# A blocked attention and two MLPs on one core: the y product three steps behind h, and small VectorE work moved to ScalarE and GpSimd

## The chip, the cores and the metric

The kernel runs on one core of a Trainium2 chip. The metric is the device time of one execution in microseconds. The core has TensorE (matmuls, and its weight loads, PE and PEld in the profile), VectorE (DVE), ScalarE (ACT), GpSimd (POOL) and SyncE (SP, which here only sends DMAs). Each engine works through its own instructions in order; semaphores order them against each other.

## The reference

```python
# q, k, v: 2 x 8 heads x 768 x 64; 8 global keys, a local window of 96
scores = scale * np.matmul(q, k.transpose(0, 1, 3, 2))
...
scores = np.where(keep, scores + bias, -1000000000.0)
scores = scores - np.max(scores, axis=-1, keepdims=True)
a = np.exp(scores)
a = a / (np.sum(a, axis=-1, keepdims=True) + 1e-09)
x = np.matmul(a, v)                    # then 1536 tokens x 512
h = x @ w_in                           # first MLP, 512 -> 2048
x = (h * np.cos(h)) @ w_out
g = x @ w_gate                         # second MLP, 512 -> 1536
out = (g * (1.0 / (1.0 + np.exp(-g))) * (x @ w_val)) @ w_out
```

`keep` lets through the global keys and those at most 95 positions back.

## The kernel before

**Numbers.** Every large product is made of three matmuls on halves: a tensor is split into a high part (a copy on ScalarE to a matmul format, `split_hi`) and a low part (what is left, a subtraction on VectorE or GpSimd, `split_lo`), and high x high, high x low and low x high are summed in PSUM. The weights come as 64-bit numbers; `narrow` makes 32-bit ones of them with three integer instructions on VectorE (L183, L186, L193), called a conversion here. A conversion is done once for each 512-column piece, the split anew for each block of tokens.

**Stages.** The tokens are in three blocks of 512. Attention of the first four tiles of 128 tokens runs alone (the prologue). The first MLP runs over 48 steps, 16 for each block; in the first 32 (`for s in range(last)`), the attention of the other eight tiles is woven in at fixed steps (`steady`, with the constants at the top of the file, `BASES` and others). What is written there is put in order on each engine by a scheduler that works before the kernel runs. From the last block of the first MLP on, the order is as written. The second MLP takes 36 steps.

**A step of the first MLP.** `h_mm(s)`: twelve matmuls into one of two PSUM buffers of tag h. `chain_a`: k, the nearest whole number of h/2pi, on ScalarE. `chain_f`: f, what is left, on VectorE (L311). `chain_sin`: sine and square on ScalarE (L320, L321). `chain_c`: the product with h, in place in PSUM, on VectorE (L328), and its high part g on ScalarE (L332). `chain_d`: the low part of g, on VectorE (L338), which is the last reader of the h buffer. `y_mm(s)`: twelve matmuls with w_out. In a step s, `h_mm(s)` comes first, then `y_mm(s - 2)`, then the chain of step s - 1. In steps 0 to 15 the weights of step s + 2 for h and of step s + 1 for y are fetched, and those of s + 2 and s converted.

**A tile of attention.** Scores, their maxima on VectorE (`scores_max`), the negated maxima (`neg_max`, L838, 128x8), exponentials with their sums on ScalarE, a split of the result (`split_p`), DMA transposes sent by SyncE (L865), the product with v (`pv`), and `x_norm`: reciprocals of the sums times v's scales (r, L899, 128x8), and the product of that with x into xn (L901). TensorE turns xn (`x_turn`, L220). In the prologue |v| is summed as well (`v_scale_part`), for the scales.

**Pools.** SBUF: `ch` holds f and k, two buffers each, `g` two buffers, `xn` one, `vr` two (v as loaded). In the second MLP, `silu` writes into f's buffers, `act` into g's, and the output tiles use k's and f's. A tile that takes a buffer waits until the last reader of the one before is done. All DMAs but one go through SyncE's queue, in order, and one that waits holds up those behind.

Of the kernel before, what the change touches and what calls it, by code (L numbers as in the profile page):

```python
# [22 lines left out]
P = 128  # L23
# [18 lines left out]
SP = (7, 7, 8, 8)  # L42
PVS = (10, 11, 11, 11)
XN = 13
XE = 15
# [8 lines left out]
E4 = 2  # L54
LAG = 2
VB = 5
VBE = 7
# [12 lines left out]
def attention_moe_moe2_kernel(  # L70
# [175 lines left out]
    def first_mlp(c1, before, steps, last_block):  # L246
# [60 lines left out]
        def chain_f(s):  # L307
            n = BLOCKS[todo[s][0]][1]
            h, k = hs[s]
            f = ch_p.tile([P, 512], F32, tag="f", name="f")  # L310
            nc.vector.scalar_tensor_tensor(  # L311
                out=f[:, :n], in0=h[:, :n], scalar=INV2PI, in1=k[:, :n],
                op0=ALU.mult, op1=ALU.subtract,
            )
            fs[s] = f
# [49 lines left out]
        def begin():  # L365
            get("i", 0)
            get("i", 1)
            get("o", 0)
            use("i", w_in, 0)
            use("i", w_in, 1)  # L370
            prep_in(0)

        before(hp, begin, prep_in, h_early)
        ch_p = c1.enter_context(tc.tile_pool(name="ch", bufs=2))
        g_p = c1.enter_context(tc.tile_pool(name="g", bufs=2))
        yp = c1.enter_context(tc.tile_pool(name="yp", bufs=4, space=PSUM))
        last = nsteps - NF1
        for s in range(last):
            early, late = steps.get(s, ((), ()))
            if s < NF1:  # L380
                get("i", s + 2)
                get("o", s + 1)
            ps = h_mm(s)
            if s >= 2:
                y_mm(s - 2)
# [8 lines left out]
            if s < NF1:  # L394
                use("i", w_in, s + 2)
                use("o", w_out, s)
            prep_out(s - 1)
            chain_a(s, ps)
# [50 lines left out]
    def second_mlp(c2, ch_p, g_p, hp, yp):  # L449
# [51 lines left out]
        def silu(s):  # L501
            n = BLOCKS[todo[s][0]][1]
            sl = ch_p.tile([P, 512], F32, tag="f", name="sl")
            nc.scalar.activation(out=sl[:, :n], in_=ps_.pop(("g", s))[:, :n], func=AF.Silu)  # L504
# [15 lines left out]
        def o_mm(s):  # L520
# [5 lines left out]
            for m in range(nt // P):  # L526
# [8 lines left out]
                if j == NF2 - 1:  # L535
                    end = b == len(BLOCKS) - 1
                    o = ch_p.tile([P, DM], F32, tag="kf"[end and m // 2], name="osb")
                    rows = slice(t0 + m * P, t0 + (m + 1) * P)
# [56 lines left out]
    def windowed_path():  # L595
# [7 lines left out]
        with ExitStack() as ca:  # L603
# [42 lines left out]
            pt_p = ca.enter_context(tc.tile_pool(name="pt", bufs=4, side="right"))  # L646
            xn_p = ca.enter_context(tc.tile_pool(name="xn", bufs=1, side="right"))
            sm_p = ca.enter_context(tc.tile_pool(name="sm", bufs=2, side="right"))
# [187 lines left out]
            def neg_max(i, p0, p1):  # L836
                c = slice(2 * p0, 2 * p1)
                nc.vector.tensor_scalar(  # L838
                    T["nm", i][:, c], T["mx", i][:, c], -1.0, P_SHIFT * LN2,
                    op0=ALU.mult, op1=ALU.add,  # L840
                )
# [49 lines left out]

            def x_norm(i):
                b = i // TB
                r = sm_p.tile([P, H], F32, tag="r", name="r")
# [3 lines left out]
                nc.vector.reciprocal(out=r, in_=r)  # L898
                nc.vector.tensor_tensor(out=r, in0=r, in1=vsc[b][:, H:2 * H], op=ALU.mult)  # L899
                xn = xn_p.tile([P, DM], F32, tag="xn", name="xn")  # L900
                nc.vector.tensor_tensor(  # L901
# [15 lines left out]
            def steady(i):  # L917
# [25 lines left out]
                for p in range(4):  # L943
                    add(SP[p] // 2, SP[p] % 2, split_p, i, p, eng(PLE, 4 * i + p), nc.scalar.copy)
                    add(PVS[p] // 2, PVS[p] % 2, pv, i, p)
                add(XN // 2, XN % 2, x_norm, i)
                add(XN // 2, L, x_tr, i)
# [22 lines left out]
            def prologue(hp, begin, prep_in, h_early):  # L970
                with (
# [31 lines left out]
                    for w in range(NW + LAG + 2):  # L1003
# [37 lines left out]
                        if 0 <= w - LAG < NW:  # L1041
                            i, pp = pairs[w - LAG]
                            pv(i, 2 * pp)
                            pv(i, 2 * pp + 1)
                            if pp == 1:
                                x_norm(i)
                        if 0 <= w - LAG - 1 < NW:
# [154 lines left out]
```

## Time and profile before

| | |
|---|---|
| time, three runs | 715.47, 719.28, 720.06 us; median 719.28 |
| profiled execution | 716.73 us, span 715.0 |
| mean granted TensorE clock | 0.972 |
| TensorE busy | 662.3 us, 93% of the span |
| VectorE busy | 483.9 us, 68% |
| ScalarE busy | 394.7 us, 55% |
| GpSimd busy | 115.3 us, 16% |

The span runs from the first to the last instruction; the profiled execution's own time lies 1.7 us above it. Busy shares are means over stages that have different limits, so they are to be read by stretch. The granted clock is a share of full speed.

### The profile page before, as it was taken

The page shows a single profiled execution, that of the slowest core. Times are in us where ns is not written, and L with a number is a line of the kernel's source. Part 1 is how long each engine was busy: PE and PEld are TensorE (multiplying, and loading weights), DVE is VectorE, ACT ScalarE, POOL GpSimd, SP SyncE. Part 2 cuts the span into 40 slices and gives each one's busy share as a digit, 9 for nine tenths or more (in the row PEclk, how much of TensorE's full clock was granted, in tenths as well). Part 3 has the DMA queues.
Part 4 walks back from the last instruction along what each step waited for, and adds up shares of the span by engine and source line. Part 5 has one row for each costly group of instructions (what it writes and reads, how often), then busy time and mean ns, then how long its engine had stood idle before and what let it go on. Part 6 is the DMA issues. An engine that isn't in the chain of part 4 may idle for free.

```text
span 715.0 us, 9068 instructions
## 1 busy us (share of the span) xinstructions
PE 662.3 (93%) x3276; PEld 521.5 (73%) x3276; DVE 483.9 (68%) x886; ACT 394.7 (55%) x820; POOL 115.3 (16%) x108
## 2 busy tenths in 40 slices
PE   4777898987898999999999999999999999999997
PEld 3345676756676777787888888888888888888885
DVE  4795999989987566747999869878443444433442
ACT  5566678777486898766666743332333333333331
POOL 2564333523322332420000000000000000000000
PEclk9996799998999999999999999999999999999999
DMA  6788546648534122300332224542000000100001
GB/s 222 190 195 211 170 132 224 172 130 201 136 104 68 37 49 45 60 1 30 102 104 89 88 59 126 161 126 88 30 30 0 1 1 0 60 0 1 1 0 63
DMA packets 69652, 62.73 MB, mean 88 GB/s; under 512 B 48896, under 2 KB 55296, under 8 KB 69600
## 3 DMA queue, kind: packets, MB, share of 16 engines
q1 hardware_dynamic: 69456, 61.95, 31.4%
q8 instruction: 27, 0.44, 0.2%
q14 instruction: 25, 0.20, 0.1%
q10 hardware_dynamic: 144, 0.13, 0.1%
HBM read 47.19 MB, written 3.15 MB: 70 GB/s over the span
## 4 chain that ended last, share of the span: by engine, by line
PE 65%; DVE 16%; ACT 10%; DMA 4%; issue 2%; POOL 1%; SPq 0%; DVEq 0%; ACTq 0%; POOLq 0%
PE v L492 14%; PE o L528 14%; PE g L492 14%; PE h L274 10%; PE y L350 10%; DMA pt<-ph 3%; ACT sb L848 3%; DVE w L193 2%; DVE w L186 2%; DVE sb L830 1%; PE s L778 1%; DVE w L183 1%; ACT L320 1%; ACT L848 1%; DVE h L328 1%
## 5 line engine op out<-in xcount | busy, mean ns | idle before, releaser
L210 DVE TENSOR_TENSOR ws<-w,ws 128x512 fp32r<-128x512 f32 x161 | 112.6, 720 | 95.1 <-ACT ws L206 94.9
L350 PE MATMUL y<-g,ws 128*128 128x512 f32 x576 | 145.8, 399 | 12.9 <-ACT g L332 11.4
L274 PE MATMUL h<-xh,ws 128*128 128x512 f32 (+1 forms) x392 | 136.3, 409 | 3.9 <-ACT xh L225 2.2
L350 PEld LDWEIGHTS y<-g,ws 128*128 128x128 f32 x576 | 109.1, 191 | 39.2 <-ACT g L332 10.9
L206 ACT CAST ws<-w 128x512 fp32r<-128x512 f32 x204 | 121.9, 615 | 21.1 <-DVE w L193 13.3
L528 PE MATMUL o<-ws,a 128*128 128x512 f32 x432 | 104.7, 391 | 0.0
L492 PE MATMUL v<-xh,ws 128*128 128x512 f32 x288 | 96.3, 395 | 0.0
L274 PEld LDWEIGHTS h<-xh,ws 128*128 128x128 f32 x392 | 77.4, 200 | 24.5 <-DVE g L338 3.6
L492 PE MATMUL g<-xh,ws 128*128 128x512 f32 x288 | 94.7, 390 | 0.0
L528 PEld LDWEIGHTS o<-ws,a 128*128 128x128 f32 x432 | 81.1, 188 | 18.4
L274 PE MATMUL h<-xl,ws 128*128 128x512 f32 (+1 forms) x196 | 78.8, 402 | 0.0
L210 POOL TENSOR_TENSOR ws<-w,ws 128x512 fp32r<-128x512 f32 x43 | 60.3, 1403 | 109.6 <-ACT ws L206 98.6
L504 ACT ACTIVATE sl<-g 128x512 f32<-128x512 f32 x36 | 21.5, 598 | 97.5 <-PE g L492 97.5
L492 PEld LDWEIGHTS v<-xh,ws 128*128 128x128 f32 x288 | 54.2, 188 | 12.7
L514 ACT CAST a<-sl 128x512 fp32r<-128x512 f32 x36 | 22.4, 622 | 72.6 <-DVE sl L510 72.6
L492 PEld LDWEIGHTS g<-xh,ws 128*128 128x128 f32 x288 | 54.1, 188 | 11.2
L492 PE MATMUL v<-xl,ws 128*128 128x512 f32 x144 | 56.9, 395 | 0.0
L492 PE MATMUL g<-xl,ws 128*128 128x512 f32 x144 | 56.0, 389 | 0.0
L193 DVE SCALAR_TENSOR_TENSOR w<-st,w 128x512 int32<-128x512 int32 x68 | 53.9, 802 | 0.8
L186 DVE SCALAR_TENSOR_TENSOR w<-st,w 128x512 int32<-128x512 int32 x68 | 48.6, 723 | 1.2
L300 ACT ACTIVATE k<-h 128x512 int32<-128x512 f32 x48 | 28.4, 592 | 34.4 <-PE h L274 34.3
L311 DVE SCALAR_TENSOR_TENSOR f<-h,k 128x512 f32<-128x512 f32 x48 | 32.9, 685 | 20.8 <-ACT k L300 20.5
(111 smaller groups left out, 821.9 us busy)
## 6 DMA issues: line engine op xcount, KB each, us to landing
st<-w1i SPq DMA_DIRECT2D x16, 512.0 KB, 3.8
st<-w1o SPq DMA_DIRECT2D x16, 512.0 KB, 4.3
st<-w2g SPq DMA_DIRECT2D x12, 512.0 KB, 3.7
st<-w2v SPq DMA_DIRECT2D x12, 512.0 KB, 3.7
st<-w2o SPq DMA_DIRECT2D x12, 512.0 KB, 3.7
vr<-v SPq DMA_DIRECT2D x16, 256.0 KB, 3.8
kr<-kT SPq DMA_DIRECT2D x12, 256.0 KB, 4.1
qr<-qT SPq DMA_DIRECT2D x12, 256.0 KB, 3.4
```

The source lines that it names most:

```text
L186: nc.vector.scalar_tensor_tensor(out=w, in0=hi, scalar=-(1 << 30), in1=w, op0=ALU.bitwise_and, op1=ALU.bitwise_or,)
L193: nc.vector.scalar_tensor_tensor(out=w, in0=lo, scalar=29, in1=w, op0=ALU.logical_shift_right, op1=ALU.bitwise_or,)
L206: nc.scalar.copy(out=s[:, 0, :], in_=w)
L210: e.tensor_tensor(out=s[:, 1, :], in0=w, in1=f32(s[:, 0, :]), op=ALU.subtract)
L274: nc.tensor.matmul(hps[s][:, c0:c1], lhsT=wis[s][:, a, k * P:(k + 1) * P], rhs=xx[:, k, t0 + c0:t0 + c1], start=(k == 0 and a == 0 and xx ...
L300: nc.scalar.activation(out=k[:, :n], in_=ps[:, :n], func=AF.Copy, scale=INV2PI)
L311: nc.vector.scalar_tensor_tensor(out=f[:, :n], in0=h[:, :n], scalar=INV2PI, in1=k[:, :n], op0=ALU.mult, op1=ALU.subtract,)
L350: nc.tensor.matmul(ys[b][m][:, :n], lhsT=w[:, a, m * P:(m + 1) * P], rhs=g[:, c, :n], start=(j == 0 and a == 0 and c == 0), stop=(j == NF1 ...
L492: nc.tensor.matmul(ps[:, :n], lhsT=w[:, a, k * P:(k + 1) * P], rhs=xx[:, k, t0:t0 + n], start=(k == 0 and a == 0 and xx is xh), stop=(k == ...
L514: nc.scalar.copy(out=a[:, 0, :n], in_=sl[:, :n])
L528: nc.tensor.matmul(os_[b][m], lhsT=a[:, c, m * P:(m + 1) * P], rhs=w[:, d, :], start=(j == 0 and c == 0 and d == 0), stop=(j == NF2 - 1 an ...
L848: nc.scalar.activation(out=a, in_=a, func=AF.Exp, bias=nm[:, h:h + 1], accum_out=sm[:, h:h + 1])
```

## The change

Five things. The y product stands three steps behind h up to step 20, where two y follow each other, and two behind from there; the loads, conversions and splits of w_out move one step back with it, and g has three buffers. f has one buffer, xn uses those of vr, `silu` those of k, and three of four output tiles those of g, the fourth that of f. `neg_max` runs on ScalarE. `x_weights` is taken out of `x_norm`, with its product on GpSimd for the eight tiles that are woven in, and stands at a step of its own, 4; in the prologue it stays on VectorE, where it was.

```diff
+RN = 8
...
+CATCH = 20
...
-            f = ch_p.tile([P, 512], F32, tag="f", name="f")
+            f = ch_p.tile([P, 512], F32, tag="f", bufs=1, name="f")
...
             get("i", 0)
             get("i", 1)
-            get("o", 0)
...
-        g_p = c1.enter_context(tc.tile_pool(name="g", bufs=2))
+        g_p = c1.enter_context(tc.tile_pool(name="g", bufs=3))
...
             if s < NF1:
                 get("i", s + 2)
-                get("o", s + 1)
+                get("o", s)
+            elif s == NF1:
+                get("o", s - 1)
             ps = h_mm(s)
-            if s >= 2:
+            if s <= CATCH:
+                if s >= 3:
+                    y_mm(s - 3)
+            if s >= CATCH:
                 y_mm(s - 2)
...
             if s < NF1:
                 use("i", w_in, s + 2)
-                use("o", w_out, s)
-            prep_out(s - 1)
+                if s >= 1:
+                    use("o", w_out, s - 1)
+            elif s == NF1:
+                use("o", w_out, s - 1)
+            if s < CATCH:
+                prep_out(s - 2)
+            if s >= CATCH - 1:
+                prep_out(s - 1)
...
-            sl = ch_p.tile([P, 512], F32, tag="f", name="sl")
+            sl = ch_p.tile([P, 512], F32, tag="k", name="sl")
...
-                    o = ch_p.tile([P, DM], F32, tag="kf"[end and m // 2], name="osb")
+                    if m < 3:
+                        o = f32(g_p.tile([P, 2, DM], F32R, tag="g", name="osb")[:, 0, :])
+                    else:
+                        o = ch_p.tile([P, DM], F32, tag="f", bufs=1, name="osb")
...
-                nc.vector.tensor_scalar(
-                    T["nm", i][:, c], T["mx", i][:, c], -1.0, P_SHIFT * LN2,
-                    op0=ALU.mult, op1=ALU.add,
+                nc.scalar.activation(
+                    out=T["nm", i][:, c], in_=T["mx", i][:, c], func=AF.Copy, scale=-1.0,
+                    bias=P_SHIFT * LN2,
                 )
...
-            def x_norm(i):
-                b = i // TB
+            def x_weights(i, e):
+
                 r = sm_p.tile([P, H], F32, tag="r", name="r")
...
                 nc.vector.reciprocal(out=r, in_=r)
-                nc.vector.tensor_tensor(out=r, in0=r, in1=vsc[b][:, H:2 * H], op=ALU.mult)
-                xn = xn_p.tile([P, DM], F32, tag="xn", name="xn")
+                e.tensor_tensor(out=r, in0=r, in1=vsc[i // TB][:, H:2 * H], op=ALU.mult)
+                T["r", i] = r
+
+            def x_norm(i):
+                r = T.pop(("r", i))
+                xn = vr_p.tile([P, DM], F32, tag="vr", name="xn")
...
+                add(RN // 2, RN % 2, x_weights, i, nc.gpsimd)
...
+                                x_weights(i, nc.vector)
                                 x_norm(i)
```

VectorE's order in the prologue, behind the low part xl of the second tile. Names end in a number for each buffer; w is a weight piece in conversion from st, r the product of reciprocals and scales, qr the queries, vm the maxima of the sums of |v|. Before:

```order
L226 TENSOR_TENSOR xl_107<-xT_629,xh_106 128x4x128
L895 TENSOR_SCALAR r_813<-sum_559 128x8
L898 RECIPROCAL r_813<-r_813 128x8
L899 TENSOR_TENSOR r_813<-r_813,vsc0_138 128x8
L901 TENSOR_TENSOR xn_723<-x_604,r_719 128x512
L695 TENSOR_TENSOR qr_77<-qr_77,hsc_109 128x512
L667 TENSOR_REDUCE vm_676<-vsum_487 128x8
```

After:

```order
L188 SCALAR_TENSOR_TENSOR w_901<-st_861,w_901 128x512
L185 TENSOR_SCALAR w_905<-st_839 128x512
L195 SCALAR_TENSOR_TENSOR w_901<-st_861,w_901 128x512
L188 SCALAR_TENSOR_TENSOR w_905<-st_839,w_905 128x512
L195 SCALAR_TENSOR_TENSOR w_905<-st_839,w_905 128x512
L909 TENSOR_SCALAR r_808<-sum_554 128x8
L912 RECIPROCAL r_808<-r_808 128x8
L709 TENSOR_TENSOR qr_77<-qr_77,hsc_109 128x512
L810 TENSOR_REDUCE mx_721<-s2_724 128x4
L919 TENSOR_TENSOR xn_718<-x_599,r_714 128x512
```

Two conversions now end ahead of xn of the third tile: a fourth piece of w_in (st_861) and the first of w_out (st_839); the first of w_out was converted a little earlier before, the fourth of w_in behind the prologue.

TensorE's order ahead of h of step 6 (h_1272 before, h_1252 after). s are scores of a woven tile; g_1205 is g of step 4, g_1110 that of step 3. Before:

```order
L755 MATMUL s_1307<-kr_76,qr_77 128x128 x2
L350 MATMUL y_942<-g_1205,ws_1217 128x512
L350 MATMUL y_943<-g_1205,ws_1217 128x512
L350 MATMUL y_944<-g_1205,ws_1217 128x512
L350 MATMUL y_945<-g_1205,ws_1217 128x512
L274 MATMUL h_1272<-xh_106,ws_1183 128x512
```

After:

```order
L769 MATMUL s_1287<-kr_76,qr_77 128x128 x2
L352 MATMUL y_981<-g_1110,ws_1197 128x512 x2
L352 MATMUL y_982<-g_1110,ws_1197 128x512 x2
L352 MATMUL y_983<-g_1110,ws_1197 128x512
L352 MATMUL y_981<-g_1110,ws_1197 128x512
L352 MATMUL y_982<-g_1110,ws_1197 128x512
L352 MATMUL y_983<-g_1110,ws_1197 128x512 x2
L352 MATMUL y_984<-g_1110,ws_1197 128x512 x2
L276 MATMUL h_1252<-xh_106,ws_1163 128x512
```

Where the four matmuls with the high part of g of step 4 stood, eleven of the twelve of step 3 stand.

SyncE's queue in the prologue, around the transposes of the third tile (pt<-ph); kr, qr, v and st are loads of keys, queries, v and weights. Before:

```order
L865 DMA_TRANSPOSE pt_502<-ph_499 128x8x128
L865 DMA_TRANSPOSE pt_507<-ph_504 128x8x128
L865 DMA_TRANSPOSE pt_594<-ph_591 128x8x128
L865 DMA_TRANSPOSE pt_599<-ph_596 128x8x128
L702 DMA vr_666<-v 128x512
L702 DMA vr_671<-v 128x512
L110 DMA kr_76<-kT 128x4x128
L865 DMA_TRANSPOSE pt_688<-ph_685 128x8x128
```

After:

```order
L879 DMA_TRANSPOSE pt_499<-ph_496 128x8x128
L879 DMA_TRANSPOSE pt_504<-ph_501 128x8x128
L176 DMA st_861<-w1i 128x1024
L716 DMA vr_572<-v 128x512
L879 DMA_TRANSPOSE pt_589<-ph_586 128x8x128
L716 DMA vr_577<-v 128x512
L879 DMA_TRANSPOSE pt_594<-ph_591 128x8x128
L112 DMA kr_76<-kT 128x4x128
L716 DMA vr_661<-v 128x512
L716 DMA vr_666<-v 128x512
L879 DMA_TRANSPOSE pt_683<-ph_680 128x8x128
```

A load of weights and two of v have come among the transposes; two more of v now stand ahead of the last one shown. vr_577 takes the buffer of the xn of the second tile, vr_666 that of vr_577.

## Rows read from the trace of the kernel before

**Rows 1.** Busy time by stretch: us; PE, PEld, DVE, ACT, POOL busy (instructions); clock, DMA share, GB/s.

```profile
75.95:195.00 119.05, 102.44 (x551) 76.66 (x550) 111.97 (x223) 88.47 (x186) 42.17 (x32) 0.92 0.61 170
195.00:345.00 150.00, 143.32 (x802) 113.02 (x802) 102.41 (x213) 116.48 (x241) 38.16 (x29) 1.00 0.23 50
345.00:715.00 370.00, 364.64 (x1591) 298.58 (x1589) 218.41 (x350) 146.76 (x260) 0.00 (x0) 1.00 0.17 53
```

**Rows 2.** Waits of TensorE, whole span: us in total, times, longest.

```profile
PE y L350 <- ACT g L332: 11.4, 7, 4.2
```

**Rows 3.** Waits of VectorE from 75 to 200 us: the same columns.

```profile
DVE w L183 <- DMA st<-w1i: 3.5, 3, 1.3
```

**Rows 4.** Groups by line to 345 us (count, busy us, mean ns); last, one line's ns min/median/max.

```profile
L899 DVE TENSOR_TENSOR r<-r,vsc 128x8 f32<-128x8 f32 x12 | 7.0, 585 | 0.1
...
L838 DVE TENSOR_SCALAR nm<-mx 128x8 f32<-128x8 f32 x7 | 2.5, 351 | 0.0
...
L311 DVE SCALAR_TENSOR_TENSOR f<-h,k x48: 674/684/693, 76.0 to 404.9; 128x512 f32<-128x512 f32 x48
```

**Rows 5.** Timeline of VectorE: start us, us, what.

```profile
81.41 1.23 DVE L838 TENSOR_SCALAR nm<-mx 128x4 f32<-128x4 f32 x1
82.55 0.68 DVE L311 SCALAR_TENSOR_TENSOR f<-h,k 128x512 f32<-128x512 f32 x1
...
136.24 1.17 DVE L838 TENSOR_SCALAR nm<-mx 128x8 f32<-128x8 f32 x1
...
157.81 0.16 DVE L838 TENSOR_SCALAR nm<-mx 128x8 f32<-128x8 f32 x1
157.88 0.76 DVE L183 TENSOR_SCALAR w<-st 128x512 int32<-128x512 int32 x2
```

**Rows 6.** Timeline of GpSimd.

```profile
81.00 1.61 POOL L210 TENSOR_TENSOR ws<-w,ws 128x512 fp32r<-128x512 f32 x1 [1.77 <-ACT ws L206]
```

**Rows 7.** ScalarE: a table load in its timeline, and its smallest copy by line.

```profile
76.44 1.28 ACT L320 ACT_TABLE_LOAD   x1
...
L685 ACT COPY kr<-gk 128x128 f32<-128x128 f32 x8 | 2.4, 295 | 5.4 <-PE s L778 5.3 <-PE s L755 0.2
```

**Rows 8.** Timeline of VectorE late in the prologue; in brackets the wait before.

```profile
56.82 0.17 DVE L895 TENSOR_SCALAR r<-sum 128x8 f32<-128x8 f32 x1 [0.69 <-ACT sb L810]
57.03 0.20 DVE L898 RECIPROCAL r<-r 128x8 f32<-128x8 f32 x1
...
61.31 0.69 DVE L901 TENSOR_TENSOR xn<-x,r 128x512 f32<-128x512 f32 x1 [3.88 <-PE x L888]
```

**Rows 9.** Timeline of VectorE amid conversions.

```profile
103.96 0.41 DVE L183 TENSOR_SCALAR w<-st 128x512 int32<-128x512 int32 x1
104.29 0.68 DVE L338 TENSOR_TENSOR g<-h,g 128x512 fp32r<-128x512 f32 x1
104.89 0.68 DVE L193 SCALAR_TENSOR_TENSOR w<-st,w 128x512 int32<-128x512 int32 x1
```

**Rows 10.** Timeline of TensorE: one y.

```profile
164.22 2.88 PE L350 MATMUL y<-g,ws 128*128 128x512 f32 x12
```

**Rows 11.** Timeline of VectorE at the end.

```profile
709.00 0.69 DVE L547 COPY osb<-o 128x512 f32<-128x512 f32 x1 [0.67 <-PE o L528]
709.68 0.42 DVE L541 COPY osb<-o 128x256 f32<-128x256 f32 x1
```

**Rows 12.** Timelines of SyncE's queue and of TensorE in the prologue.

```profile
46.00 6.38 SPq L865 DMA_TRANSPOSE pt<-ph  x4
52.44 1.05 SPq L702 DMA_DIRECT2D vr<-v  x2
...
54.35 1.58 SPq L865 DMA_TRANSPOSE pt<-ph  x1
...
50.40 0.64 PE L220 MATMUL xT<-ident,xn 128*128 128x128 f32 x4
```

**Rows 13.** DMA issues by line: KB each, median us to landing.

```profile
vr<-v SPq DMA_DIRECT2D x16, 256.0 KB, 3.8
```

More of the change, by code (lines that the diff above doesn't have):

```diff
@@ L646, in windowed_path @@
             pt_p = ca.enter_context(tc.tile_pool(name="pt", bufs=4, side="right"))
-            xn_p = ca.enter_context(tc.tile_pool(name="xn", bufs=1, side="right"))
             sm_p = ca.enter_context(tc.tile_pool(name="sm", bufs=2, side="right"))
```

## The prediction

> **What bounds the kernel now.** I first cut the span into three stretches [rows 1]. From 75.95 us, where the chain of the first step begins on VectorE, to 195 us, VectorE is busy 111.97 of 119.05 us and TensorE 102.44, at a mean granted clock of 0.92. From 195 to 345 us TensorE is busy 143.32 of 150 us at full clock. Behind 345 us it is busy 364.64 of 370, and the rest is the end of the program. So the change can win only in the first stretch, where VectorE sets the pace, in the 6.7 us that TensorE still waits in the second, and ahead of 75.95 us. The waits of TensorE seem to say otherwise: its longest are for g, 11.4 us in seven waits, the longest 4.2 us [rows 2]. But g is the end of the chain k, f, sine, square, c, g, d, and three of its links run on VectorE. h has two PSUM buffers, and c and d work in them, so h of step s cannot begin before d of step s - 2 is through. Between the end of h(s-2) and the start of h(s), TensorE has one y, one h and one y to do whether y is two steps behind or three; the lag decides only which y that is. A later y is a filler for a short stall, but it does not let the chain start sooner.
>
> VectorE's own losses in the first stretch are of two kinds. It waits for weights, 3.5 us in three waits [rows 3]. And some of its small instructions last far longer than they need: the negation of the maxima has a mean of 351 ns and the product r a mean of 585 ns [rows 4], although an undisturbed negation holds VectorE for 0.07 us (157.81 to 157.88) [rows 5]. A negation that began at 81.41 lasted 1.23 us, to 82.64, and GpSimd worked on a split from 81.00 to 82.61 [rows 5, 6]. Another lasted 1.17 us at 136.24. With two products there are four such in the stretch, each of some 1.1 us more than it needs. By the same views VectorE's f, which reads PSUM and one SBUF tile, never lasts longer than 693 ns [rows 4].
>
> **The change part by part.** The sum is made for the profiled execution, 716.73 us (span 715.0 and 1.7 around it).
>
> *Small work off VectorE.* Eight negations and eight of the twelve products leave. In the first stretch there are four and three of these. Three are short, together 0.3 us by the 0.07 to 0.16 us that one holds the engine. The four long ones hold it 1.14 us each (81.41 to 82.55) [rows 5], 4.6 us together. Whether that is won depends on the instruction behind: where f follows, as behind 81.41, it would not have waited; where the first step of a conversion follows, as behind 136.24, it may wait in the place of the negation. The trace has two of each. I take half, -2.3, with ends at 0 and -4.6.
> The Trainium skill ("SBUF — State Buffer", Who interferes with whom) calls the pair of ports that VectorE and GpSimd share an exclusive lock, held for the whole instruction, and says that a VectorE instruction with two SBUF inputs contends with a GpSimd instruction that reads SBUF. By that rule the eight products, now GpSimd's, take the lock themselves, and a wait that leaves with a small instruction can pass to the next; the sum by it is the second rival below. The trace agrees as to the waits: the instructions of [rows 5, 6] end within 0.03 us of each other.
>
> *What they cost where they go.* No row shows a 128x8 copy on ScalarE. Bounds are the 295 ns of its 128x128 copy [rows 7] from above and zero from below; eight make at most 2.4 us. Two table loads more stand in ScalarE's order (12 and 11 against 11 and 10), 1.28 us each [rows 7]: 2.6 us, both in the first stretch. ScalarE is idle for 30.6 us there and for 33.5 us in the second [rows 1], so I set all of this at nothing; without that cover it would cost up to 5.0 us. On GpSimd, idle for 76.9 us of the first stretch, the product stands some two steps ahead of the xn that needs it: nothing again, and at most 1.6 us for one that lands behind a split [rows 6], which steps of 8.5 us (some fourteen in the stretch) hide.
>
> *Weights.* Loads and conversions of w_out move one step back; those of w_in keep their step, and so run ahead. The order of VectorE has five conversions finished at the first f, where four stood before. The one gained runs where VectorE now waits, 3.88 us ahead of xn at 61.31 [rows 8], and costs nothing there. It takes out of the first stretch its three instructions, 0.33 and twice 0.60 us by the starts at 103.96, 104.29 and 104.89 [rows 9]: -1.5. If the weights land too late for that place, it is 0.
>
> *One buffer for f.* f(s) must now wait for c(s-1). The order before has them so anyway except at the first pair. What is left is that VectorE waits for its own result: an instruction that does so starts 0.04 us behind the end of the one before (56.82 + 0.17 to 57.03) [rows 8], others start 0.08 us ahead of it (104.29 + 0.68 to 104.89) [rows 9], so 0.12 us. Four of the first sixteen f stand right behind their c: +0.5; all sixteen would be +1.9.
>
> *The lag.* At h(17), where the first stretch is over, the order of TensorE has fifteen y done and a third of another before, and exactly fifteen after: four matmuls are carried into the stretch that TensorE fills. Twelve take 2.88 us [rows 10], so +0.9. With the two y of step 20 the rest of the order is as before.
>
> *Output tiles and xn.* At the end of each block of tokens the third output tile now takes the buffer of g that the last matmuls still read. In the last block its copy must wait for the very last matmul; before, it ran at 709.00, and the half copy behind it began with the last matmul at 709.68 [rows 11]. The end moves by that copy, +0.7. At the two earlier block ends TensorE has other work queued. xn now shares two buffers with the loads of v, so a load of v waits until TensorE has turned an xn, and everything on SyncE's queue waits with it. Of the four transposes from 46.00, at 1.6 us each, the fourth went at about 50.8; in the new order a load that needs the turn of 50.40 to 51.04 stands ahead of it, and takes 0.5 us itself (two loads in 1.05), so it goes at about 51.6 [rows 12]. Against that, a cast and a subtraction for v leave VectorE's part of the prologue for a later place. I set the prologue at 0, from -1 to +4 (third rival).
>
> The sum: -0.3 - 2.3 - 1.5 + 0.5 in the first stretch, +0.9 in the second, +0.7 at the end: -2.0 us. The four executions shown lie at 715.47, 716.73, 719.28 and 720.06; the profiled one is 2.55 below the median of the three runs. I put the sum to the middle of the four, 718.0: **716.0 us**.
>
> **The rivals.** *Everything that VectorE waits for goes.* All four long instructions end (-2.3 more) and the 3.5 us for weights too, since w_in is fetched a step ahead of w_out: -2.0 - 5.8 = -7.8, 710.2 us. For it speaks that the order of GpSimd changes too, and with it which instructions meet; against it that GpSimd does the same splits as before and will meet others. 0.2.
> *The lock passes on.* The -2.3 is lost, and the products on GpSimd hold VectorE three times for as long as VectorE's own short one, 0.16 us: -2.0 + 2.3 + 0.5 = +0.8, 718.8 us. For it speaks that two of the four long ones have a conversion behind them, all of whose inputs are in SBUF. 0.2.
> *SyncE's queue stops for xn: slower.* Two loads of v, one behind a turn of xn and one behind the sum of |v| that ScalarE takes of the first, stand ahead of transposes in the prologue. The first costs 0.8 us as above, and 2.4 if the third transpose is pushed behind it too (51.6 against 49.2). The second goes only when the first has landed, 3.8 us later [rows 13], and been taken up by ScalarE, which needs more than the 0.3 us of its smaller copy [rows 7], say 0.6; with 0.5 for itself its transpose is at about 56.0 and not at 54.35: 1.6. -2.0 + 4.0 = +2.0, 720.0 us. It decides from the point at which a turn ends later than the GpSimd split that the transpose waits for; splits bind there too, which speaks against the whole price. 0.15.
>
> **How the numbers follow.** The forecast, 714 to 718, has 0.45. The range reaches past the first rival and past the third, by some of a run's own spread, 2.3 us about the middle: 709 to 723. A change of 1% (7.2 us) is what a measurement of this kernel can tell from none. Faster than 712.1: the first rival, 0.2. Slower than 726.5 needs the third with all other gains lost: 0.05. Within 1%: 0.75.
>
> **What would show it.** Right: in the changed profile VectorE is still the fullest engine between 75 and 190 us; small instructions on it above 1 us are at most half as many; d(15) comes 3 to 4 us earlier against d(0); five conversions are done ahead of the first f; the last matmul and the end are 0.7 us further apart. Wrong: TensorE's waits for g fall and VectorE's busy time does not follow (then the lag had been the bound); the first f comes later than 78 us (SyncE's queue); conversions now last longer than 1 us where negations did (the lock); or ScalarE's idle time in the first stretch is gone.

## The result, and the profile after

| | before | changed |
|---|---|---|
| time, four runs each | 717.96 us (715.47 to 720.06) | 707.92 us (707.24 to 710.14) |
| profiled execution, span | 716.73, 715.0 | 708.31, 706.5 |
| ratio | 1 | 0.9881, 95% interval 0.9857 to 0.9904 |

By the ratio the change takes 8.5 us off, 6.9 to 10.3 (the medians of four runs each lie 10.0 us apart). The sum was -2.0 against 718.0: the sign was right and the size a quarter of what came. 707.92 is nearest to the first rival's 710.2 and 1.1 us under the low end of the range; that it is not that rival's mechanism is shown below.

Where the 8.5 us of the two spans lie is read from five points: the first g (its low part, d of step 0), d of step 15, d of step 47, the last matmul, the end. The starts of d in VectorE's timeline are 85.62, 213.0 and 408.31 before and 83.16, 205.77 and 398.40 after. So the prologue with the first chain is 2.5 us shorter, steps 0 to 15 4.8, steps 15 to 47 2.7, and the end lies 1.35 us further behind the last matmul. From d of step 47 to the last matmul every kernel profiled here takes 301.3 to 301.4 us.

Busy time of the changed kernel by the stretches of [rows 1]:

```profile
75.95:195.00 119.05, 102.67 (x571) 76.97 (x570) 109.99 (x228) 93.57 (x198) 41.28 (x36) 0.94 0.60 168
195.00:345.00 150.00, 145.38 (x817) 115.87 (x816) 102.70 (x205) 118.63 (x249) 38.95 (x33) 1.00 0.25 56
345.00:706.50 361.50, 354.79 (x1548) 290.43 (x1546) 209.45 (x335) 141.00 (x250) 0.00 (x0) 1.00 0.16 52
```

VectorE is still the fullest engine of the first stretch, as forecast, and five conversions (where four stood) end ahead of the first f. But a stretch fixed in time hides what is gained in it, so here is the way from the first to the sixteenth d by itself, in the same columns; first the kernel before:

```profile
85.62:213.00 127.38, 112.98 (x608) 85.48 (x607) 116.70 (x240) 95.86 (x210) 42.38 (x32) 0.94 0.57 157
```

and the changed one:

```profile
83.16:205.77 122.61, 110.23 (x603) 83.07 (x604) 110.31 (x226) 98.95 (x216) 41.84 (x37) 0.96 0.57 157
```

VectorE's busy time falls by 6.4 us, its idle time rises from 10.7 to 12.3. The granted clock was 0.96 on this way and 0.94 before, and TensorE was busy for 2.75 us less, so some 2.5 of the 4.8 us (2% of the way, an estimate) may be the clock of these two executions. What TensorE waits for from 75 to 345 us in the changed kernel (line waited for: us in total, times, longest):

```profile
PE s L769 <- DVE mx L844: 5.9, 4, 2.3
PE y L352 <- DVE ws L212: 3.4, 4, 1.6
PE y L352 <- ACT ws L208: 3.4, 4, 2.6
PE h L276 <- DVE g L340: 2.9, 4, 1.2
```

The wait of y for g, 11.4 us of the whole span before [rows 2], is gone, and waits of y for the split weights and of the scores for maxima have come. VectorE's largest wait from 75 to 200 us is as long as before [rows 3]:

```profile
DVE w L185 <- DMA st<-w1i: 3.5, 2, 2.8
```

At the end of the program the third output tile is now copied behind the last matmul, as forecast (VectorE's timeline, against [rows 11]):

```profile
699.83 0.69 DVE L562 COPY osb<-o 128x512 f32<-128x512 f32 x1 [1.35 <-PE o L540]
700.44 0.41 DVE L556 COPY osb<-o 128x256 f32<-128x256 f32 x1
```

Last, the first f starts 2.4 us earlier than before (75.95 in [rows 1]'s first column):

```profile
73.58 0.69 DVE L313 SCALAR_TENSOR_TENSOR f<-h,k 128x512 f32<-128x512 f32 x1 [0.41 <-ACT k L302]
```

### The profile page after: what moved, and what is told of

It reads as the page before. It is cut to its first block, busy times and chain, and to the rows that moved or that the text cites. A ratio compares the mean times of both kernels' runs of the same rounds, so it can differ in the third digit from the quotient of the medians.

```text
span 706.5 us, 9076 instructions
## 1 busy us (share of the span) xinstructions
PE 659.3 (93%) x3276; PEld 520.2 (74%) x3276; DVE 475.1 (67%) x870; ACT 398.5 (56%) x830; POOL 115.7 (16%) x116
## 4 chain that ended last, share of the span: by engine, by line
PE 70%; ACT 14%; DVE 9%; DMA 3%; issue 2%; POOL 1%; DVEq 0%; SPq 0%; POOLq 0%; ACTq 0%
PE v L504 14%; PE o L540 14%; PE g L504 14%; PE h L276 11%; PE y L352 11%; ACT sb L862 3%; DMA pt<-ph 3%; PE s L769 2%; PE s L792 2%; ACT L322 1%; ACT ws L208 1%; ACT k L302 1%; ACT L862 1%; ACT ph L876 1%; PE x L902 1%
## 5 line engine op out<-in xcount | busy, mean ns | idle before, releaser
L212 DVE TENSOR_TENSOR ws<-w,ws 128x512 fp32r<-128x512 f32 x161 | 110.3, 706 | 96.6 <-ACT ws L208 95.3
L276 PE MATMUL h<-xh,ws 128*128 128x512 f32 (+1 forms) x392 | 133.1, 401 | 3.0 <-DVE g L340 2.9
L276 PEld LDWEIGHTS h<-xh,ws 128*128 128x128 f32 x392 | 75.6, 195 | 23.5 <-DVE g L340 4.9
L276 PE MATMUL h<-xl,ws 128*128 128x512 f32 (+1 forms) x196 | 77.4, 395 | 0.0
L330 DVE SCALAR_TENSOR_TENSOR h<-f,h 128x512 f32<-128x512 f32 x48 | 33.2, 691 | 22.9 <-ACT f L323 22.8
```

The lines of the kernel that those rows point to most:

```text
L212: e.tensor_tensor(out=s[:, 1, :], in0=w, in1=f32(s[:, 0, :]), op=ALU.subtract)
L276: nc.tensor.matmul(hps[s][:, c0:c1], lhsT=wis[s][:, a, k * P:(k + 1) * P], rhs=xx[:, k, t0 + c0:t0 + c1], start=(k == 0 and a == 0 and xx ...
L330: nc.vector.scalar_tensor_tensor(out=h[:, :n], in0=f[:, :n], scalar=0.5, in1=h[:, :n], op0=ALU.subtract, op1=ALU.mult,)
```

## The experiments

Ratios are against runs of the kernel before on the same chip. "First d" and the ways between are from one profiled execution of each; that of the pools alone was its slowest (717.23 us), those with late w_out (714.07) and with the small work put back (707.11) were their fastest.

| | median us | ratio (95%) | first d | d0 to d15 | d15 to d47 | last matmul to end |
|---|---|---|---|---|---|---|
| before | | 1 | 85.62 | 127.38 | 195.31 | 5.36 |
| changed | 707.92 | 0.9881 (0.9857, 0.9904) | 83.16 | 122.61 | 192.63 | 6.71 |
| small work alone | 714.19 | 0.9951 (0.9934, 0.9969) | 85.95 | 124.85 | 195.35 | 6.01 |
| small work put back | 707.87 | 0.9879 (0.9857, 0.9902) | 78.18 | 123.74 | 194.80 | 6.89 |
| pools alone | 714.94 | 0.9955 (0.9936, 0.9973) | 81.21 | 126.80 | 199.53 | 6.46 |
| pools, late w_out | 718.06 | 1.0017 (1.0000, 1.0034) | 77.35 | 129.12 | 198.05 | 6.39 |
| pools, lag | 713.89 | 0.9956 (0.9937, 0.9974) | 78.71 | 129.56 | 195.19 | 6.85 |
| xn's buffers alone | 708.95 | 0.9887 (0.9852, 0.9922) | 79.17 | 125.67 | 197.07 | 5.25 |

**1. The small work alone.** The kernel before, with

```diff
-                nc.vector.tensor_scalar(
-                    T["nm", i][:, c], T["mx", i][:, c], -1.0, P_SHIFT * LN2,
-                    op0=ALU.mult, op1=ALU.add,
+                nc.scalar.activation(
+                    out=T["nm", i][:, c], in_=T["mx", i][:, c], func=AF.Copy, scale=-1.0,
+                    bias=P_SHIFT * LN2,
...
+                add(RN // 2, RN % 2, x_weights, i, nc.gpsimd)
```

> The kernel before with the small work alone moved: negated maxima on ScalarE, the product r of the woven tiles on GpSimd at a step of its own. Pools, lag and the timing of w_out as before. Theory V (VectorE sets the pace up to the sixteenth step, and what is won is VectorE's time): 3 to 5 us faster than before, VectorE's busy time between the first and the sixteenth g shorter by 3 to 5 us, and TensorE's waits for g in y stay near 11 us in total. Theory L (the lag wins: the waits of y for g, 11.4 us before, were what held TensorE): 0 to 2 us faster, and those waits unchanged.

Measured: 3.5 us faster (2.2 to 4.7), the time of Theory V. The way from the first to the sixteenth d in its trace:

```profile
85.95:210.80 124.85, 112.96 (x608) 86.15 (x608) 109.01 (x229) 93.43 (x209) 42.08 (x37) 0.92 0.59 160
```

VectorE's busy time is 7.7 us less than before, and the way only 2.5 us shorter; the other 5.1 us have become idle time of VectorE (15.8 against 10.7). The granted clock was 0.92 here and 0.94 before; 2% of this way are 2.5 us, too little to make up for them. So VectorE is not by itself what sets the pace there. Waits of y for g stay (11.0 us from 75 to 345 us).

**2. The small work put back** in the changed kernel, everything else as changed.

```diff
-                nc.scalar.activation(
-                    out=T["nm", i][:, c], in_=T["mx", i][:, c], func=AF.Copy, scale=-1.0,
-                    bias=P_SHIFT * LN2,
+                nc.vector.tensor_scalar(
+                    T["nm", i][:, c], T["mx", i][:, c], -1.0, P_SHIFT * LN2,
+                    op0=ALU.mult, op1=ALU.add,
...
             def x_norm(i):
+                x_weights(i, nc.vector)
                 r = T.pop(("r", i))
...
-                add(RN // 2, RN % 2, x_weights, i, nc.gpsimd)
```

> The changed kernel with the small work put back: negated maxima and the product r on VectorE where they stood before. Lag of three, late w_out and the pools as changed. Theory V: 2 to 4 us faster than before (the start of the first step some 2.4 us earlier as in the changed kernel, and one conversion less in the first stretch), the way from the first to the sixteenth g shorter by 1 to 2 us only. Theory L: 7 to 9 us faster, as the changed kernel, with no wait of y for g.

Measured: 0.9879, the whole gain. Theory V falls. Its start is even earlier (first d 78.18); the small work takes 3.3 us from the steps (318.5 us from the first to the last d here, 315.2 in the changed kernel), and the first d comes 5.0 us later with it (83.16). TensorE's waits from 75 to 345 us:

```profile
PE y L352 <- DVE ws L212: 6.2, 3, 2.5
PE h L276 <- DVE g L340: 6.2, 5, 1.8
PE y L352 <- ACT ws L208: 2.9, 3, 2.0
...
PE y L352 <- ACT g L334: 0.5, 2, 0.2
```

**3. No lag.** The changed kernel with y two steps behind and w_out in its old place.

```diff
-            if s <= CATCH:
-                if s >= 3:
-                    y_mm(s - 3)
-            if s >= CATCH:
+            if s >= 2:
                 y_mm(s - 2)
...
-                get("o", s)
...
+                get("o", s + 1)
...
-            if s < CATCH:
-                prep_out(s - 2)
-            if s >= CATCH - 1:
-                prep_out(s - 1)
+                use("o", w_out, s)
+            prep_out(s - 1)
```

> The changed kernel with y two steps behind h throughout and the loads, conversions and splits of w_out where they stood before; pools and small work as changed. Theory V: 2 to 4 us slower than the changed kernel (one conversion more in the first stretch, the start of the first step as before), so some 6 us faster than before. Theory L: the waits of y for g are back at 8 us or more and with them all but 1 or 2 us of the gain: within 2 us of before.

Measured: 714.23 us, ratio 0.9957 (0.9932 to 0.9982): most of the gain is gone. The waits of y for g are back, but with 6.3 us. The 3.1 us that are left lie between the two theories.

**4. The third output tile** of the last block in a buffer of k.

```diff
-                    if m < 3:
+                    if m == 2 and end:
+                        o = ch_p.tile([P, DM], F32, tag="k", name="osb")
+                    elif m < 3:
```

> The changed kernel, with the third output tile of the last block in a buffer of k and not in the buffer of g that the last matmuls read. Everything else as changed. If the 1.35 us that the end lies further behind the last matmul than before (6.71 against 5.36 us) come from this buffer: the copy ahead of the half copies starts 0.7 us earlier, and the time falls by 0.7 to 1.3 us against the changed kernel, to some 707. If not: no change.

Measured: the end lies 5.65 us behind the last matmul in place of 6.71, so the buffer cost 1.06 us. The ratio, 0.9859 (0.9834 to 0.9885), agrees and cannot settle it alone.

**5. The pools alone** on the kernel before: xn, f, g, `silu` and the output tiles as in the change's diff.

```diff
+            f = ch_p.tile([P, 512], F32, tag="f", bufs=1, name="f")
...
+        g_p = c1.enter_context(tc.tile_pool(name="g", bufs=3))
...
+                xn = vr_p.tile([P, DM], F32, tag="vr", name="xn")
```

> The kernel before with the pools alone as changed: xn in the two buffers of the loads of v, one buffer for f, three for g, silu in k, the output tiles in g and f. Lag, timing of w_out and small work as before. Theory W (the late w_out wins: its first load no longer stands among the transposes of the prologue, its conversions leave the first stretch): within 1.5 us of before. Theory X (xn with two buffers shortens the prologue): 2 to 4 us faster, the first f 2 to 3 us earlier. Theory L (the lag): within 1.5 us of before.

Measured: 0.9955, 3.2 us faster; the first f at 74.24, 1.7 us earlier. Theory X as to the time.

**6. Pools and late w_out, without the lag.** The small work is put back as in experiment 2; besides, against the changed kernel:

```diff
             ps = h_mm(s)
-            if s <= CATCH:
-                if s >= 3:
-                    y_mm(s - 3)
-            if s >= CATCH:
+            if s >= 2:
                 y_mm(s - 2)
...
-            if s < CATCH:
-                prep_out(s - 2)
-            if s >= CATCH - 1:
-                prep_out(s - 1)
+            prep_out(s - 1)
```

> The pools as changed and loads, conversions and splits of w_out one step later (the split of a piece in the step ahead of its y), but y two steps behind h throughout; small work as before. Theory W: 6 to 9 us faster than before, the first g some 5 to 7 us earlier. Theory X: 2 to 4 us faster. Theory L: at most 2 us faster, waits of y for g at 8 us or more.

Measured: 1.0017, 4.4 us worse than the pools alone. The first d is the earliest of all (77.35), and all that it gains is lost behind it. Theory W falls as it was put. y waits for g 9.1 us from 75 to 345 us, as Theory L had it.

**7. Pools and the lag, w_out in its old place.** Against the kernel before, besides the pools:

```diff
-            if s >= 2:
+            if s <= CATCH:
+                if s >= 3:
+                    y_mm(s - 3)
+            if s >= CATCH:
                 y_mm(s - 2)
...
                 use("o", w_out, s)
             prep_out(s - 1)
```

> The pools as changed and y three steps behind h up to step 20, but loads, conversions and splits of w_out where they stood before; small work as before. Theory L: 6 to 9 us faster than before, no wait of y for g. Theory W: at most 2 us faster. Theory X: 2 to 4 us faster, as the pools alone.

Measured: 0.9956, the same as the pools alone, and y waits for g 8.5 us. Theory L falls as it was put. Neither half of the lag wins anything by itself; together they take the pools from 0.9955 to 0.9879, 5.5 us (3.4 to 7.5 with both intervals).

**8. The small work put back, and the tile of experiment 4:** both edits together.

```diff
+                    if m == 2 and end:
+                        o = ch_p.tile([P, DM], F32, tag="k", name="osb")
...
+                x_weights(i, nc.vector)
                 r = T.pop(("r", i))
```

> The lag, the late w_out and the pools of the changed kernel, the small work back on VectorE (as in the run that put it back), and the third output tile of the last block in a buffer of k. If the two effects add: 1.0 us less than with the small work put back, 706.8 us, 10.5 us faster than before; its end 5.4 to 5.7 us behind the last matmul. Its prologue is that of the run with the small work put back, so its first f shows whether 70.1 us there was one execution's luck: at 70 to 71 us if the order sets it, at 73 or later if it was.

Measured: 707.59 us, ratio 0.9852 (0.9827 to 0.9878), the lowest of all, not clear of the changed kernel. Its end lies 5.5 us behind the last matmul, as expected. Its first f is at 71.47 us, between the two places named, and its first d at 79.90, so most of the early start of experiment 2 was there again.

**9. and 10. Which part of "late" the lag needs.** Pools and lag, with only the splits of w_out a step later (9) or only its loads and conversions (10). In both the small work is put back; besides, against the changed kernel, (9), where the loads too stand as before:

```diff
-                if s >= 1:
-                    use("o", w_out, s - 1)
-            elif s == NF1:
-                use("o", w_out, s - 1)
+                use("o", w_out, s)
```

and (10):

```diff
-            if s < CATCH:
-                prep_out(s - 2)
-            if s >= CATCH - 1:
-                prep_out(s - 1)
+            prep_out(s - 1)
```

> Pools and the lag of three as changed, small work as before. Loads and conversions of w_out where they stood before; only the splits of w_out come one step later, as in the changed kernel. Theory S (what the late w_out adds to the lag is that TensorE's order really follows: with early splits the scheduler pulls y ahead again, 15.3 y done at the eighteenth h and 18.3 at the twenty-first as against 15.0 and 17.0): 7 to 9 us faster than before, waits of y for g under 3 us. Theory C (it is the conversion that leaves VectorE's early steps): 2 to 4 us faster, as the pools with the lag alone.

> Pools and the lag of three as changed, small work as before. Loads and conversions of w_out one step later as changed, but its splits right behind the conversion, in the same step, two steps ahead of their y. Theory C: 7 to 9 us faster than before. Theory S: 2 to 5 us faster, waits of y for g at 5 us or more, since y is pulled ahead (16.3 y done at the twentieth h, 18.3 at the twenty-first).

Measured: 0.9913 (0.9882 to 0.9944) and 0.9924 (0.9901 to 0.9946), each about half way from 0.9956 to 0.9879. Theory S is right on its sign: with late splits y follows the lag in TensorE's order (15.0 y done at the eighteenth h). The waits of (9) from 75 to 345 us:

```profile
PE h L276 <- DVE g L340: 9.8, 9, 2.5
PE s L765 <- DVE mx L840: 2.7, 1, 2.7
PE y L352 <- ACT g L334: 2.1, 3, 1.1
```

With early splits and late conversions the scheduler has pulled y ahead (15.3), and it waits for g as long as before:

```profile
PE y L352 <- ACT g L334: 11.4, 7, 5.7
PE h L276 <- DVE g L340: 6.2, 5, 1.8
```

But this kernel gains too, 2.3 us against experiment 7 (0.2 to 4.4). With the splits alone 2.4 us of the whole gain are missing, which the intervals do not settle (-0.3 to 5.2). So both parts seem to count, and neither theory covers both; how the gain is shared is not shown.

**11. xn's buffers alone**, on the kernel before:

```diff
-            xn_p = ca.enter_context(tc.tile_pool(name="xn", bufs=1, side="right"))
...
-                xn = xn_p.tile([P, DM], F32, tag="xn", name="xn")
+                xn = vr_p.tile([P, DM], F32, tag="vr", name="xn")
```

> The kernel before with xn alone in the two buffers of the loads of v. If what the pools win comes from this buffer: 2 to 4 us faster than before, as the pools alone, the transposes of the third tile (46.00 before) some 2.5 us earlier, the first f at 72 to 74.5 us. If it comes from another pool: within 1 us of before. If the rival of the prediction holds in another place (a load of v waits for a turn): 1 to 4 us slower.

Measured: 708.95 us, ratio 0.9887 (0.9852 to 0.9922), 8.1 us faster. That is more than any of the three cases expected, and as much as the whole change, but in another place: the first d comes 6.5 us earlier (79.17), and behind it the way to d of step 47 is the old one (322.74 us, 322.69 before). SyncE's queue in its prologue, to be read against [rows 12]:

```profile
37.89 1.07 SPq L701 DMA_DIRECT2D vr<-v  x2
...
41.76 3.93 SPq L864 DMA_TRANSPOSE pt<-ph  x2
45.75 0.57 SPq L174 DMA_DIRECT2D st<-w1o  x1
46.42 0.37 SPq L701 DMA_DIRECT2D vr<-v  x1
46.84 1.25 SPq L864 DMA_TRANSPOSE pt<-ph  x1
49.97 0.33 SPq L701 DMA_DIRECT2D vr<-v  x1
50.40 1.24 SPq L864 DMA_TRANSPOSE pt<-ph  x1
...
53.20 1.59 SPq L864 DMA_TRANSPOSE pt<-ph  x1
```

The loads of v do stand among the transposes, as the third rival had it, and the fourth transpose gains little (50.40 against 51.10). But the first of the four goes at 41.76 and not at 46.00, the next tile's first at 53.20 and not 54.35, and its last at 60.52 and not 63.72. Three of these stand inside merged rows; here they are alone, the first two from the kernel before:

```profile
51.10 1.29 SPq L865 DMA_TRANSPOSE pt<-ph  x1
63.72 1.23 SPq L865 DMA_TRANSPOSE pt<-ph  x1
60.52 1.26 SPq L864 DMA_TRANSPOSE pt<-ph  x1
```

ScalarE's timeline of the kernel before shows what stood ahead of the first of the four: eight exponentials and a sum of |v| ahead of the tile's first split.

```profile
39.49 0.47 ACT L810 ACTIVATE sb<-s,nm 128x256 f32<-128x256 f32 x1 [3.11 <-DVE nm L800]
...
41.31 0.64 ACT L660 ACTIVATE va<-vr 128x512 fp32r<-128x512 f32 x1
...
44.10 1.18 ACT L862 CAST ph<-sb 128x512 f16<-128x512 f32 x2
```

With the shared buffers the split comes behind four exponentials, and the sum behind the split:

```profile
39.18 0.48 ACT L809 ACTIVATE sb<-s,nm 128x256 f32<-128x256 f32 x1
...
40.09 1.17 ACT L861 CAST ph<-sb 128x512 f16<-128x512 f32 x2
41.23 0.63 ACT L659 ACTIVATE va<-vr 128x512 fp32r<-128x512 f32 x1
```

Two loads of v that stood at 23.20 us in SyncE's queue before now stand at 37.89, and what hangs on them gives way to the tiles that the first f needs. The first f comes at 72.62, 3.3 us earlier; the other 3.1 us of the earlier first d lie between the two (6.55 us, 9.67 before), where VectorE is held for less: the conversions that follow the first f take 3.22 us before and 1.53 here, and the negation 1.23 [rows 5] and 0.15.

```profile
76.56 3.22 DVE L193 SCALAR_TENSOR_TENSOR w<-st,w 128x512 int32<-128x512 int32 x2
73.22 1.53 DVE L193 SCALAR_TENSOR_TENSOR w<-st,w 128x512 int32<-128x512 int32 x1
```

**12. The negated maxima alone** on ScalarE, product and all else as before.

```diff
-                nc.vector.tensor_scalar(
-                    T["nm", i][:, c], T["mx", i][:, c], -1.0, P_SHIFT * LN2,
-                    op0=ALU.mult, op1=ALU.add,
+                nc.scalar.activation(
+                    out=T["nm", i][:, c], in_=T["mx", i][:, c], func=AF.Copy, scale=-1.0,
+                    bias=P_SHIFT * LN2,
```

> The kernel before with the negated maxima alone on ScalarE. If the gain of the small work (some 3 us for both) is that of the long instructions taken off VectorE: two of the four long ones were negations, so 1 to 2 us faster. If it is all the negation's, because ScalarE's exponentials no longer wait for VectorE: 2.5 to 4 us faster. If it is all the product's on GpSimd: within 1 us.

Measured: 714.48 us, ratio 0.9959 (0.9936 to 0.9981), 2.9 us (1.4 to 4.6): within the intervals all that the small work wins, though 1 to 2 us are not excluded.

## Why the prediction was right and wrong

**What bounds the kernel.** The prediction took the stretch's fullest engine for the one that sets the pace. Experiment 1 refutes the simple form of that: 7.7 us less busy time on VectorE, 2.5 us less way. The first stretch is a chain through three engines, and time freed on one was mostly waited away. Its sign for being wrong, that the waits for g fall and VectorE's busy time does not follow, did not show: both fell in the changed kernel, and only taking the parts asunder told them apart. In the changed kernel's one profile the four stretches came out at -2.5 us ahead of the first d (forecast 0), -4.8 from there to d of step 15 (-3.6), -2.7 to d of step 47 (+0.9) and +1.35 at the end (+0.7).

**Output tiles and xn, "I set the prologue at 0".** Of all terms, each taken by itself, this one was furthest off. All kernels with xn in v's buffers have their first d at 77.4 to 83.3 us, the three without it (before, experiments 1 and 12) at 85.6 to 86.2. By itself, with xn in these buffers and no other edit, it is worth 8.1 us (5.6 to 10.6); with the rest of the change around it 2.5 us come ahead of the first d. The third rival priced the waits that it puts into SyncE's queue, on the order printed; it did not ask what no longer runs early when loads of v have to wait. Its waits are there, and near their price in the changed kernel: the fourth transpose of the third tile goes at 51.61 (priced 51.6), the next tile's first at 56.72 (56.0). But that tile's last goes at 61.49 in place of 63.72, so the gain elsewhere is larger. The 50.8 and 49.2 that the prediction read from the merged row for the kernel before are 51.10 and 49.77.

**The lag, +0.9, and the weights, -1.5.** Costed as two terms with a price each, they have none: lag alone 0 (within 1.9 either way), late weights alone 4.4 us slower (2.6 to 6.2), both 5.5 us faster, each time against the pools. The argument that a later y fills no gap that an earlier one does not fill held as long as y really stands where its weights let it: with early splits the scheduler has 15.3 y done at the eighteenth h in either case. It missed that a late y lets its weights be late, and that late weights without a late y are a loss.

**One buffer for f, +0.5.** The pools alone are 4.9 us slower than xn's buffers alone (2.1 to 7.7), of which some 1.2 is the end (6.46 against 5.25). The rest is with f, g, `silu` and the order that they give; these were not separated. In the trace of the pools alone f of the second step starts at 80.61, behind the product of the first (79.60); with xn alone it starts at 76.63, ahead of it (77.23). So f waits at the "first pair", as the prediction said, but the way from the first f to the first d is only 0.4 us longer there (6.97 against 6.55); 1.6 us come ahead of the first f and 3.6 behind the first d. That f's buffer carries the loss is not shown.

**The small work, -2.6.** Its size was near where it stands alone: 3.5 us. With the lag, late w_out and pools it wins nothing more (0.9881 against 0.9879), and with the pools without lag neither (0.9957 against 0.9955). The second rival, that a wait leaves with a small instruction and passes to the next, may be seen in part. In the changed kernel a low part of v and one of a tile's exponentials, of 0.68 us each undisturbed, last 1.7 us (VectorE):

```profile
79.90 1.71 DVE L732 TENSOR_TENSOR vs<-vr,vs 128x512 f16<-128x512 f32 x1
...
173.79 1.74 DVE L877 TENSOR_TENSOR ph<-sb,ph 128x512 f16<-128x512 f32 x1
```

and GpSimd works on a split from 79.79 and from 173.70:

```profile
79.79 1.26 POOL L212 TENSOR_TENSOR ws<-w,ws 128x512 fp32r<-128x512 f32 x1 [2.93 <-ACT ws L208]
...
173.70 1.29 POOL L212 TENSOR_TENSOR ws<-w,ws 128x512 fp32r<-128x512 f32 x1 [1.58 <-ACT ws L208]
```

They end at 81.05 and 174.99, and VectorE's instructions 0.5 to 0.6 us later. Both of them read two SBUF tiles, and the Trainium skill ("SBUF — State Buffer", Who interferes with whom) names that form as one that contends; here the trace agrees. In the conversions of weights the waits did not grow: their three instructions take 56.4 us of the first stretch (76 of them), 57.9 before (77). The prediction looked at the small instructions alone: over 1 us lasted, in the first stretch, 22 instructions of VectorE before, 16 of them in conversions, and 17 after, 13 of them in conversions. So its sign for the lock, conversions above 1 us, could not tell. That two of the four long waits went on, the half that it took, fits these counts and is not shown. What failed is the step from VectorE's time to the kernel's.

```profile
L913 POOL TENSOR_TENSOR r<-r,vsc 128x8 f32<-128x8 f32 x8 | 2.9, 358 | 10.4 <-DVE r L912 7.8 <-ACT ph L876 2.6
...
L852 ACT ACTIVATE nm<-mx 128x8 f32<-128x8 f32 x7 | 1.5, 209 | 2.8 <-DVE mx L844 2.7
```

The products cost GpSimd 2.9 us in all. The negation costs ScalarE 0.21 us, under the 0.3 that bounded it, and ScalarE's idle time in the first stretch is still 25.5 us (119.05 less 93.57).

**The end, +0.7.** The mechanism was right, the size not: 1.35 us, of which experiment 4 takes back 1.06.

**The first rival** gives nearly the time and is not what happened: VectorE waits for weights 3.5 us as before, and without the small work moved the time is the same.

So the sign came from a sum whose largest true term was set at nothing, and was in so far luck; the forecast gain was too small for that reason, and because terms that work only in company were priced alone.

**Open.** Why the late weights need the late y to win; whether f's single buffer, g's third or the order costs the pools what xn's buffers win; and whether xn's buffers with the negated maxima on ScalarE, and nothing else, would beat experiment 8. None of this was tried.

## What to carry to other kernels

Where a scheduler sets the order, a shared buffer is also a statement of priority: look at what it pushes back, not only at the waits that it adds. Price parts that need each other (a product a step later, its weights a step later) as one, and test them in pairs: here each alone was worth nothing or less. And an engine that is busy 94% of a stretch need not set its pace; measure by taking work off it alone.

## What the runs showed of the hardware that was not expected

The changed kernel's profiled execution had the lower granted clock in the prologue and yet the earlier start: 0.73 up to the first d, against 0.87 before. In both executions of the order with the small work moved and w_out late that were profiled (the changed kernel and experiment 4), TensorE ran at 0.50, its lower level of 1.2 GHz, from 40 to 50 us and was busy 9.87 and 9.74 of those 10 us; in experiment 2 it was granted 1.00 there and was busy 8.02 us.

```profile
40.00:50.00 10.00, 9.87 (x51) 5.60 (x50) 7.08 (x13) 6.64 (x21) 5.30 (x4) 0.50 0.98 236
```

Whether that is why the small work's first d is 5 us later there is not shown. It is not the small work's doing alone: with the small work on VectorE the pools alone and xn's buffers alone were granted 0.64 and 0.54 in these 10 us. Among the kernels with xn in v's buffers, those granted 1.00 there (experiments 2 and 6 to 10) have their first d at 77.4 to 79.9 us, those granted 0.50 to 0.64 (the changed kernel, experiments 3, 4, 5 and 11) at 79.2 to 83.3, so what the order and what the clock of one execution gives to the first d is not told apart.

Over a whole run the mean granted clock lay between 0.950 and 0.987. Within the 59 runs of the kernel before it goes with the time only loosely: the four longest, 719.86 to 720.36 us, are all at 0.955 and the shortest, 714.66, is at 0.962, but 719.57 came at 0.968. In the six runs with xn's buffers alone the two go together throughout, from 706.29 us at 0.970 to 714.36 at 0.954. So part of the spread between runs of one kernel goes with the clock, and the profile of one execution has to be read with its own.
